# Sharing the rows of w_out over the DMA engines in another way, in a decode block of cached attention and gMLP

## The chip, the cores and the metric

One core of a Trainium2 chip runs the whole program. Its engines are TensorE (PE in the profile, with its weight loads as PEld), VectorE (DVE), ScalarE (ACT), GpSimd (POOL) and SyncE (SP, which here does nothing but issue transfers). Transfers between HBM and the core's SBUF run on 16 DMA engines. SP, ACT and GpSimd put transfers into queues; each transfer is cut into packets, and each DMA engine works off its own share of them in order. The metric is the time of one execution on the device in microseconds; lower is better.

## What is computed

```python
def _A_ref(x, k_cache, v_cache, wq, wo):
    q = (x @ wq).reshape(B, Sq, H, Dh).transpose(0, 2, 1, 3)
    scores = jnp.einsum('bhqd,bhkd->bhqk', q, k_cache) * Dh ** (-0.5)
    p = _softmax(scores, axis=-1)
    o = jnp.einsum('bhqk,bhkd->bhqd', p, v_cache)
    return o.transpose(0, 2, 1, 3).reshape(B, Sq, H * Dh) @ wo

def _B_ref(x, w_in, w_sp, b_sp, w_out):
    z = _gelu(jnp.einsum('bsd,df->bsf', x, w_in))
    z1 = z[..., :Fh]
    z2 = _layernorm(z[..., Fh:], axis=-1)
    g = jnp.einsum('ts,bsf->btf', w_sp, z2) + b_sp[None, :, None]
    return jnp.einsum('bsf,fd->bsd', z1 * g, w_out)

xn = _layernorm(x, axis=-1)
return x + _A_ref(xn, k_cache, v_cache, wq, wo) + _B_ref(xn, w_in, w_sp, b_sp, w_out)
```

Four sequences (B = 4) of one new token each (Sq = 1), D = 640, 32 heads of 128, 4096 cached positions; the gMLP has Fh = 864. All inputs and the output are bf16. The caches are 4 x 32 x 4096 x 128 elements each, 134 MB for K and as much for V; wq and wo are 5.2 MB each, w_in 2.2 MB, w_out (864 rows of 640 elements, 1280 B a row) 1.1 MB.

## The kernel before

The heads are taken in four groups of eight, and a unit is one group of one sequence: 16 units of K and 16 of V, each 128 partitions of 65,536 B (8.4 MB). A big SBUF tile `kv` has five slots of half a unit. The units follow one another in the order of `seq`: four K units first, then V and K in turn, and each load (`load_unit`, L174 to L181) is issued by SP as soon as what lay in its slots has been read. SP works through its list in order, so a load that waits holds back all loads behind it.

A K unit goes through eight steps of `emit_K`: VectorE transposes an eighth of it into one half of `w_words` (L425), TensorE multiplies it with the queries in `QZ` (L436). After four K units comes a softmax (L481 to L501), and then the V units (`emit_V`, L503 to L526): 64 matmuls each (L509), a masking and a sum on VectorE. Each group's result goes through a selection matmul (L531) and is multiplied with its quarter of wo (`o_mul`, L548 to L553). The sum over groups, the residual and the gMLP's result gather in one PSUM tile, `proj`; the last quarter's later part goes into `last`, and both are added for the output (L617).

At the start, SP issues wq (L119), w_in (L122) and w_out; then the first K unit. w_out does not come in one piece. `FA` = 3 rows lie on each of the 128 partitions (`w_out`, L126 and L127: two rows and one row, 8 partitions a DMA engine, so 24 rows an engine). The other 480 rows lie in `w_rest`, which is a view of `w_words` that VectorE first clears (L128), as up to `FR` = 17 rows on a few partitions. The table `PC` (L61) lists these pieces: first and last partition, rows a partition, and `k`, the number of groups into which the source's outermost axis is put. A transfer is spread over as many DMA engines as its groups allow, and `load_piece` (L131) uses that: piece 0 is 200 rows in five groups, piece 1 is 144 rows in three, both issued by SP; piece 2 is 136 rows in two groups and is issued by GpSimd. Just before piece 2, GpSimd issues a transfer of 14 short runs in seven groups into a tile `walk` that nobody reads (L141); `tc.issue_after` keeps the two in that order. [...] What the engines carry of w_out is therefore uneven: three have 112 rows, two 64, two 92, nine 24.

The gMLP runs while the first K unit is on its way. Its 864 columns are laid out in `FC` = `FA` + `FR` = 20 chunks of up to 128, in the same order as the rows of w_out: `z_ps` takes the first three chunks (L338, L339), `zr_ps` the pieces (L343), both for all five parts `c` of D. ScalarE applies gelu (L349 for the chunks, L357 and L360 for the pieces), VectorE and GpSimd normalise (L371 to L389), VectorE transposes (L390), and TensorE adds 2 x 20 products to `proj` (L403). `w_words` then becomes the place of the K transposes.

At the end SP issues the remaining quarters of wo (L570 to L572): the second and the third in one transfer each, the last in five.

```python
load_wo(NG - 3)
load_wo(NG - 2)
load_wo(NG - 1, (0, 2, 4, 6, 7, 8))
```

After them, `emit_proj` multiplies the second and third quarter (L591 to L595; the third in two halves, L593 and L595), and L599 to L614 the last.

The loads of SP and ACT share eight completion semaphores in turn. A load waits until the load that had its semaphore before it has landed.

Of the kernel before, what the change touches and what calls it, by code (L numbers as in the profile page):

```python
# [8 lines left out]
ACT = mybir.ActivationFunctionType  # L9
ALU = mybir.AluOpType  # L10
AX = mybir.AxisListType
F32 = mybir.dt.float32
BF16 = mybir.dt.bfloat16
# [3 lines left out]
def kernel(  # L17
# [19 lines left out]
    nc = tc.nc  # L37
    P = 128
    B, Sq, D = A_x.shape
    _, H, Sk, Dh = A_k_cache.shape  # L40
    assert Sq == 1 and B == 4 and Dh == P and D % P == 0
    DC = D // P
# [9 lines left out]
    NG = H // HG  # L52
# [1 line left out]
    G = HG * B  # L54
    F2 = B_w_in.shape[1]
    Fh = F2 // 2
    FA = 3
    FR = 17
    nf = FA * P

    PC = ((0, 20, 10, 5), (32, 44, 12, 3), (60, 68, 17, 2))  # L61
    f_at = [nf]
    for p0, p1, n, _ in PC:
        f_at.append(f_at[-1] + (p1 - p0) * n)
    assert Fh == f_at[-1]
    FC = FA + FR
    NOUT = A_wo.shape[1]
# [5 lines left out]
    const = ctx.enter_context(tc.tile_pool(name="const", bufs=1))  # L73
# [12 lines left out]
    def misc_ps(shape, dtype):  # L86
        misc_ctr[0] += 1
        return ps_m.tile(shape, dtype, tag="misc", name=f"misc{misc_ctr[0]}")
# [5 lines left out]
    n_p = (2 * TC + 1) * 16  # L94
    w_words = const.tile([P, max(2 * NKT + n_p, FR * NOUT // 2)], F32, name="w_words")
    kT_t = w_words[:, 0:2 * NKT].rearrange("p (i n) -> p i n", i=2)
    pT_t = w_words[:, 2 * NKT:2 * NKT + n_p].bitcast(BF16).rearrange("p (j r) -> p j r", r=32)

    def at_slot(i, n, off=0):
        return kv[:, i * SL + off:i * SL + off + n]  # L100
# [22 lines left out]

    w_out = at_slot(2, FA * NOUT, n_in).rearrange("p (c n) -> p c n", c=FA)

    nc.sync.dma_start(out=w_out[:, 0:2], in_=B_w_out[0:2 * P, :].rearrange("(p c) n -> p c n", p=P))  # L126
    nc.sync.dma_start(out=w_out[:, 2:3], in_=B_w_out[2 * P:nf, :].rearrange("(p c) n -> p c n", p=P))  # L127
    nc.vector.memset(w_words[:, 0:FR * NOUT // 2], 0.0)  # L128
    w_rest = w_words[:, 0:FR * NOUT // 2].bitcast(BF16).rearrange("p (c n) -> p c n", c=FR)

    def load_piece(eng, t):  # L131
        p0, p1, n, k = PC[t]
        return eng.dma_start(out=w_rest[p0:p1, 0:n].rearrange("p c n -> p (c n)"),
                             in_=B_w_out[f_at[t]:f_at[t + 1], :].rearrange("(r i c) n -> i r (c n)", i=k, c=n))

    NST = 256
    walk = const.tile([14, NST], BF16)

    load_piece(nc.sync, 0)
    load_piece(nc.sync, 1)  # L140
    sw = nc.gpsimd.dma_start(out=walk, in_=B_w_out[0:14, 0:NST].rearrange("(r i) n -> i r n", i=7))  # L141
    with tc.issue_after(sw.ins):
        load_piece(nc.gpsimd, 2)

    NB = 32 * FC
    z_at = n_in + FA * NOUT

# [26 lines left out]
    def load_unit(item):  # L174
        key, u = item
        g, b = divmod(u, B)
        cache = A_k_cache if key == "k" else A_v_cache
        src = cache[b, g * HG:(g + 1) * HG].rearrange("e (m t) d -> (e m) (t d)", t=T)
        c = cuts.get(item, (0, T))
        for t0, t1 in zip(c[:-1], c[1:]):  # L180
            nc.sync.dma_start(out=unit(item, t0, t1), in_=src[:, t0 * Dh:t1 * Dh])  # L181
# [5 lines left out]
    def load_wo(g, c_cuts=(0, HG)):  # L187
        for c0, c1 in zip(c_cuts[:-1], c_cuts[1:]):
            nc.sync.dma_start(out=wo_t[g][:, c0:c1, :], in_=wo_q[g][:, c0:c1, :])  # L189
# [30 lines left out]
    xnT = const.tile([P, DC, 32], BF16)  # L220
# [43 lines left out]
    for q in range(4):  # L264
        nc.gpsimd.tensor_copy(out=SelE[32 * q:32 * q + 32, :, q % 2, :],
                              in_=b8[32 * q:32 * q + 32, 8:8 + HP, None].to_broadcast((32, HP, P // HG)))
# [10 lines left out]
                          in_=ident_f[:].rearrange("p (q x c) -> p q x c", q=2, c=C2))  # L277
# [12 lines left out]
    for hf in range(NH):  # L290
        nc.tensor.matmul(proj[0:32, 0:NO2], lhsT=ident_bf[:XR, 1 - hf:33 - hf],
                         rhs=x_bf[:, hf * NO2:(hf + 1) * NO2], start=(hf == 0), stop=False)
# [4 lines left out]
    for hf in range(2):  # L297
        for c in range(DC):
            for j in range(NG):
                n0 = j * HG * Dh + hf * 512  # L300
                nc.tensor.matmul(q4_ps[32 * j:32 * j + 32, hf * 512:hf * 512 + 512], lhsT=xnT[:, c, :],  # L301
                                 rhs=wq[:, c, n0:n0 + 512], start=(c == 0), stop=(c == DC - 1))
# [12 lines left out]


    w_z = w_in.rearrange("p c (a f) -> p c a f", a=2)
    z_ps = misc_ps([P, 2, FA, 32], F32)
    zr_ps = misc_ps([P, 2, 256], F32)


    z_in = [[], [], [], []]
    for t, (p0, p1, n, k) in enumerate(PC):
        src = w_z[:, :, :, f_at[t]:f_at[t + 1]]
        for q in range(p0 // 32, (p1 - 1) // 32 + 1):
            x0, x1 = max(p0, 32 * q), min(p1, 32 * q + 32)
# [3 lines left out]
            else:  # L330
                src_q = src
            z_in[q].append((t, x0 - 32 * q, x1 - 32 * q, src_q))
    z_of = [[sum((x1 - x0) * PC[t][2] for t, x0, x1, _ in z[:m]) for m in range(len(z) + 1)] for z in z_in]
    w_z2 = w_z[:, :, :, 0:2 * P].rearrange("p c a (q j i) -> p c q a i j", q=4, j=32)
    w_z1 = w_z[:, :, :, 2 * P:nf].rearrange("p c a (q j) -> p c q a j", q=4)
    for c in range(DC):
        for q in range(4):
            nc.tensor.matmul(z_ps[32 * q:32 * q + 32, :, 0:2], lhsT=xnT[:, c, :], rhs=w_z2[:, c, q], start=(c == 0), stop=False)  # L338
            nc.tensor.matmul(z_ps[32 * q:32 * q + 32, :, 2], lhsT=xnT[:, c, :], rhs=w_z1[:, c, q], start=False,  # L339
                             stop=(c == DC - 1))  # L340
        for q in range(4):
            for m, (_, _, _, src) in enumerate(z_in[q]):
                nc.tensor.matmul(zr_ps[32 * q:32 * q + 32, :, z_of[q][m]:z_of[q][m + 1]], lhsT=xnT[:, c, :], rhs=src[:, c],  # L343
                                 start=(c == 0 and m == 0), stop=(c == DC - 1 and m == len(z_in[q]) - 1))
    z_f = at_slot(2, 2 * 3 * NB, z_at).bitcast(F32).rearrange("p (a n) -> p a n", a=3)
    z_b = at_slot(2, 2 * NB, z_at + 6 * NB).rearrange("p (a n) -> p a n", a=2)
    zT = z_f[:, 0:2, :].rearrange("p a (i j) -> p a i j", j=32)
    nc.gpsimd.memset(z_f[:, 0:2, :], 0.0)
    nc.scalar.activation(out=zT[:, :, 0:FA, :], in_=z_ps[:], func=ACT.Gelu_apprx_tanh)  # L349
    for q in range(4):  # L350
        rows = slice(32 * q, 32 * q + 32)
        for m, (t, x0, x1, _) in enumerate(z_in[q]):
            p0, p1, n, k = PC[t]
            z = zr_ps[rows, :, z_of[q][m]:z_of[q][m + 1]]
            dst = zT[rows, :, FA:FA + n, x0:x1]
            if x1 - x0 < p1 - p0:
                nc.scalar.activation(out=dst, in_=z.rearrange("p a (x c) -> p a c x", c=n), func=ACT.Gelu_apprx_tanh)  # L357
            else:
                for a in range(2):
                    nc.scalar.activation(out=dst[:, a].rearrange("p c (i r) -> p c i r", i=k),  # L360
                                         in_=z[:, a].rearrange("p (r i c) -> p c i r", i=k, c=n), func=ACT.Gelu_apprx_tanh)
# [36 lines left out]
    for f0 in range(0, FC, 4):  # L398
        for hf in range(NH):
            for fc in range(f0, min(f0 + 4, FC)):  # L400
# [3 lines left out]
                                 rhs=(w_out[:, fc] if fc < FA else w_rest[:, fc - FA])[:, hf * NO2:(hf + 1) * NO2],  # L404
                                 start=(fc == 1 and hf == 0), stop=False)
# [122 lines left out]
    def emit_sel(g):  # L528

        ox = misc_ps([P, B, P // HG, HG], F32)  # L530
        nc.tensor.matmul(ox[:].rearrange("p b q c -> p (b q c)"), lhsT=SelX[:].rearrange("p h q -> p (h q)"),  # L531
                         rhs=state["R"][:].rearrange("p b d -> p (b d)"), start=True, stop=True)
        om = ppool.tile([P, B, P // HG, HG], F32, tag="p", name="om")
        nc.vector.tensor_tensor(out=om[:], in0=ox[:], in1=MkQ[:, None, :, None].to_broadcast((P, B, P // HG, HG)), op=ALU.mult)
        state[("om", g)] = om
# [19 lines left out]
    def emit_proj(g, h2=range(2), close=False):  # L555
        for h in h2:
            for hf in range(NH):
                for c in range(4 * h, 4 * h + 4):
                    o_mul(proj[32 * (c % 2):32 * (c % 2) + 32], g, c, hf, hf * NO2, (hf + 1) * NO2, False,
                          close and c == HG - 1 and hf == NH - 1)  # L560

    fill_qz(0)
    for i, item in enumerate(seq):
        if i + 1 < len(seq):
            key, u = seq[i + 1]
            load_unit(seq[i + 1])
            if key == "k" and u == 2 * B - 1:
                load_wo(u // B - 1)
        else:
            load_wo(NG - 3)  # L570
            load_wo(NG - 2)
            load_wo(NG - 1, (0, 2, 4, 6, 7, 8))  # L572
        key, u = item
        g, b = divmod(u, B)
        if key == "k":
            done = b == B - 1 and g > 0
            for k in range(8):
                emit_K(u, k)
                if done and k == 1:
                    emit_sel(g - 1)  # L580
                if done and k == 2:
                    emit_oT(g - 1)
                if done and k == 5 and g == 1:
                    emit_proj(g - 1)
            if b == B - 1:
                if g < NG - 1:
                    fill_qz(g + 1)
                softmax(g)
        else:
            emit_V(u)  # L590
# [58 lines left out]
```

## Time and profile before

| | |
|---|---|
| median of 3 runs | 663.54 us (663.45 to 664.74) |
| the profiled execution | 663.36 us, of which the span on the engines is 661.6 us |
| busy in the span | VectorE 377.3 us (57%), TensorE 281.7 (43%), ScalarE 73.9 (11%), GpSimd 70.3 (11%) |
| first K load (L181) issued, landed | 17.95 us, 45.52 us |
| gMLP's products (L403) | 38.68 to 43.87 us |
| first K transpose (L425) | 45.74 us |
| K and V loads, issue to landing | 27.6 / 30.5 / 44.2 us (least, median, most) |
| TensorE clock granted, mean | 0.755 |

A page of the profile has six parts: busy times, the span in 40 slices, the DMA queues, the chain of work that ended last, the costliest groups of instructions, and the transfers. In the first part the shares are of the span. In the DMA part, q1 is SP's queue, q10 ScalarE's and q0 GpSimd's; q8 and q14 bring instructions to the engines. The chain of waits starts at the last instruction and goes back, at each step to what released it; in order of time its lines give start, duration and what it was. A row of the window table gives start and end, length, the busy time of each engine with its number of instructions, and at its end the granted clock, the busy share of the 16 DMA engines and GB/s.

### The profile page before, as it was taken

What the parts mean: (1) busy time and instruction counts of PE and PEld (TensorE: products, weight loads), DVE (VectorE), ACT (ScalarE), POOL (GpSimd) and SP (SyncE); (2) the same over time, 40 slices, a digit from 0 to 9 for tenths busy, and PEclk for the clock granted to TensorE, in tenths of its full rate; (3) what the DMA queues carried; (4) which work ended last, traced back from release to release, by engine and by line L of the source; (5) the groups of instructions that cost most, each with busy time, mean ns of one, the idle gap of its engine ahead of it and who ended that gap; (6) DMA issues with size and microseconds to landing.
All of it is one profiled execution on the core that took longest, in us unless ns stands there. A gap on an engine that the chain in (4) does not pass through costs nothing.

```text
span 661.6 us, 5513 instructions
## 1 busy us (share of the span) xinstructions
PE 281.7 (43%) x2293; PEld 106.9 (16%) x2293; DVE 377.3 (57%) x307; ACT 73.9 (11%) x143; POOL 70.3 (11%) x138
## 2 busy tenths in 40 slices
PE   0445555437052455334435075532606245652236
PEld 0221111112011121111112021110202112120012
DVE  4329989766191758718346196864629175971112
ACT  0300000330100000340200000070110000043200
POOL 3620000030200000130300000030020000003300
PEclk9868879778687697677759677875867778666779
DMA  8999999999999999999999999999999999999997
GB/s 367 458 421 440 425 436 445 436 421 440 421 436 437 444 405 436 441 441 436 433 420 428 437 422 445 442 425 432 432 433 432 433 440 411 446 432 429 423 423 286
DMA packets 7276, 282.60 MB, mean 427 GB/s; under 512 B 929, under 2 KB 1324, under 8 KB 1836
## 3 DMA queue, kind: packets, MB, share of 16 engines
q1 hardware_dynamic: 7112, 282.07, 98.9%
q8 instruction: 18, 0.29, 0.2%
q0 software_dynamic: 112, 0.18, 0.1%
q14 instruction: 6, 0.05, 0.0%
q10 hardware_dynamic: 28, 0.01, 0.0%
HBM read 282.25 MB, written 0.01 MB: 427 GB/s over the span
## 4 chain that ended last, share of the span: by engine, by line
DMA 74%; DVE 12%; issue 11%; PE 2%; ACT 0%; SPq 0%; DVEq 0%; ACTq 0%
DMA kv<-in_A_k_cache_dram 63%; DVE w_words L425 11%; DMA kv<-in_A_v_cache_dram 5%; DMA kv<-in_A_wo_dram 3%; DMA kv<-in_A_wq_dram 3%; PE O L509 1%; DVE w_words L491 0%; PE S L436 0%; DVE Zb L469 0%; DVE m L443 0%; PE last L552 0%; ACT p_bf L485 0%; SPq L189 0%; PE proj L552 0%; PE misc L447 0%
## 5 line engine op out<-in xcount | busy, mean ns | idle before, releaser
L425 DVE STREAM_TRANSPOSE w_words<-kv 128x2048 f32<-128x2048 f32 x128 | 282.8, 2275 | 127.2 <-DMA kv<-in_A_k_cache_dram 127.2
L436 PE MATMUL S<-w_words,QZ 128*32 128x512 bf16 x1024 | 183.3, 490 | 262.5 <-DVE w_words L425 262.5
L436 PEld LDWEIGHTS <-QZ 128*32 128x32 bf16 x1024 | 59.2, 110 | 384.3 <-issue 318.1
L509 PE MATMUL O<-kv,Zb 128*32 128x512 bf16 x1024 | 72.0, 443 | 57.6 <-DMA kv<-in_A_v_cache_dram 51.1
L473 ACT ACTIVATE Zb<-w_words,MkE 32x128 bf16<-32x128 bf16 x120 | 60.9, 508 | 117.2 <-PE O L509 103.3
L518 DVE TENSOR_TENSOR om<-O,Mk 128x512 f32<-128x512 f32 x15 | 10.4, 692 | 92.1 <-PE O L509 92.1
L471 POOL TENSOR_SCALAR Zb<-w_words,MkE 32x128 bf16<-32x128 bf16 x60 | 43.3, 722 | 138.6 <-PE O L509 118.0
L485 ACT ACTIVATE p_bf<-S,negmax 128x1024 bf16<-128x1024 f32 x4 | 4.5, 1114 | 401.5 <-DVE negmax L453 401.5
L509 PEld LDWEIGHTS <-Zb 128*32 128x32 bf16 x1024 | 33.3, 110 | 96.1 <-issue 66.5
L469 DVE TENSOR_SCALAR Zb<-w_words,MkE 32x128 bf16<-32x128 bf16 x76 | 24.9, 327 | 2.3
L411 POOL COPY QZ<-qT 32x32 bf16<-32x32 bf16 x16 | 5.0, 315 | 184.9 <-PE S L436 184.3
L519 DVE TENSOR_REDUCE R<-om 128x128 f32<-128x512 f32 x15 | 15.3, 1020 | 0.5
L496 POOL TENSOR_SCALAR rs<-MkB,rowsum 128x4 f32<-128x4 f32 x4 | 1.2, 296 | 112.2 <-ACT p_bf L485 112.2
L491 DVE STREAM_TRANSPOSE w_words<-p_bf 128x1024 bf16<-128x1024 bf16 (+1 forms) x8 | 9.6, 1240 | 5.9 <-ACT p_bf L485 4.1
L542 POOL MEMSET oT<- 128x66 bf16 x4 | 0.5, 146 | 98.0 <-PE proj L552 98.0
L443 DVE TENSOR_REDUCE m<-S 128x1 f32<-128x1024 f32 x4 | 4.9, 1224 | 6.1 <-PE S L436 6.1
L521 DVE TENSOR_SCALAR R<-O,Mk 128x128 f32<-128x128 f32 x1 | 0.4, 351 | 13.0 <-PE O L509 13.0
L531 PE MATMUL misc<-R,SelX 128*128 128x512 f32 x8 | 4.5, 644 | 7.2 <-DVE R L519 5.5
L301 PE MATMUL q<-kv,xnT 128*32 128x512 bf16 x40 | 4.5, 631 | 6.4 <-DVE xnT L222 6.4
L498 PE MATMUL misc<-rs,SelE 128*128 128x4 f32 x8 | 2.3, 364 | 10.4 <-POOL rs L496 10.4
L552 PE MATMUL proj<-kv,oT 128*8 128x320 bf16 x52 | 5.6, 352 | 1.2 <-DMA kv<-in_A_wo_dram 1.2
L128 DVE MEMSET w_words<- 128x5440 f32 x1 | 4.6, 4592 | 1.9 <-issue 1.9
(107 smaller groups left out, 87.9 us busy)
## 6 DMA issues: line engine op xcount, KB each, us to landing
kv<-in_A_k_cache_dram SPq DMA_DIRECT2D x8, 4096.0 KB, 30.2
kv<-in_A_v_cache_dram SPq DMA_DIRECT2D x1, 6144.0 KB, 28.6
kv<-in_A_wq_dram SPq DMA_DIRECT2D x1, 5120.0 KB, 17.2
kv<-in_A_wo_dram SPq DMA_DIRECT2D x3, 1280.0 KB
kv<-in_B_w_in_dram SPq DMA_DIRECT2D x1, 2160.0 KB, 22.7
kv<-in_A_v_cache_dram SPq DMA_DIRECT2D x1, 2048.0 KB
kv<-in_A_wo_dram SPq DMA_DIRECT2D x3, 320.0 KB, 22.7
kv<-in_B_w_out_dram SPq DMA_DIRECT2D x1, 320.0 KB, 23.0
```

Of the source, the lines that this page charges most:

```text
L411: nc.gpsimd.tensor_copy(out=QZ[r0:r0 + 32, :, :, :, 8 + 8 * hp], in_=qT[32 * g:32 * g + 32, NE * hp:NE * hp + NE].rearrange("p e a b -> p ...
L425: nc.vector.transpose(kT.rearrange("p (t r) -> p t r", r=32), kw)
L436: nc.tensor.matmul(S_ps[32 * q:32 * q + 32, i], lhsT=QZ[:, b, 2 * kh + w, e, w0:w0 + 32], rhs=kb[:, i, :, e, :, w], start=(b == 0 and k < ...
L443: nc.vector.tensor_reduce(out=m1[:], in_=S_ps[:].rearrange("p i t m -> p (i t m)"), axis=AX.X, op=ALU.max)
L469: nc.vector.tensor_scalar(out=dst, in0=src, scalar1=mk, scalar2=None, op0=ALU.mult)
L471: nc.gpsimd.tensor_scalar(out=dst, in0=src, scalar1=mk, scalar2=None, op0=ALU.mult)
L473: nc.scalar.activation(out=dst, in_=src, func=ACT.Copy, scale=mk)
L491: nc.vector.transpose(pT_t[:, j0:j1, :], blocks)
L509: nc.tensor.matmul(O_ps[32 * q:32 * q + 32, :, :], lhsT=Zb[b % 2][:, w].rearrange("p h c -> p (h c)"), rhs=vv[:, w * 4 * Dh:(w + 1) * 4 * ...
L518: nc.vector.tensor_tensor(out=om4[:], in0=O_ps[:], in1=Mk4[:, :, None].to_broadcast((P, 4, Dh)), op=ALU.mult)
L519: nc.vector.tensor_reduce(out=R, in_=om4[:].rearrange("p c d -> p d c"), axis=AX.X, op=ALU.add)
L552: nc.tensor.matmul(dst[0:nb, 0:n1 - n0], lhsT=state[("oT", g)][:, c0:c0 + nb], rhs=wo_t[g][:, c, n0:n1], start=start, stop=stop)
```

## The change

Two rows of w_out instead of three lie on each partition, in one load instead of two: 16 rows an engine. The other 608 rows are cut in another way. Pieces 0 and 1 are both 220 rows in five groups, on SP's queue; piece 2 is 120 rows in two groups on GpSimd's. A fourth piece of 48 rows on three partitions follows on GpSimd's queue, after a second walk of 12 short runs in six groups. Its source is written as two halves. The gMLP then has 18 chunks instead of 20, and the tiles that depend on it become narrower. The pieces' columns of `z` are put into `zr_ps` for pieces 0 and 1 and behind the first chunks in `z_ps` for the others. The third quarter of wo is loaded in two halves.

```diff
-    FA = 3
-    FR = 17
+    FA = 2
+    FR = 16
...
-    PC = ((0, 20, 10, 5), (32, 44, 12, 3), (60, 68, 17, 2))
+    PC = ((0, 20, 11, 5), (32, 52, 11, 5), (60, 68, 15, 2), (124, 127, 16, 1))
...
-    nc.sync.dma_start(out=w_out[:, 0:2], in_=B_w_out[0:2 * P, :].rearrange("(p c) n -> p c n", p=P))
-    nc.sync.dma_start(out=w_out[:, 2:3], in_=B_w_out[2 * P:nf, :].rearrange("(p c) n -> p c n", p=P))
+    nc.sync.dma_start(out=w_out, in_=B_w_out[0:nf, :].rearrange("(p c) n -> p c n", p=P))
...
-        return eng.dma_start(out=w_rest[p0:p1, 0:n].rearrange("p c n -> p (c n)"),
-                             in_=B_w_out[f_at[t]:f_at[t + 1], :].rearrange("(r i c) n -> i r (c n)", i=k, c=n))
+        src = B_w_out[f_at[t]:f_at[t + 1], :]
+        src = src.rearrange("(r i c) n -> i r (c n)", i=k, c=n) if k > 1 else src.rearrange("(h c) n -> h (c n)", h=2)
+        return eng.dma_start(out=w_rest[p0:p1, 0:n].rearrange("p c n -> p (c n)"), in_=src)
...
+    walk2 = const.tile([12, NST], BF16)
...
-        load_piece(nc.gpsimd, 2)
+        p78 = load_piece(nc.gpsimd, 2)
+    with tc.issue_after(p78.ins):
+        sw2 = nc.gpsimd.dma_start(out=walk2, in_=B_w_out[0:12, 0:NST].rearrange("(r i) n -> i r n", i=6))
+    with tc.issue_after(sw2.ins):
+        load_piece(nc.gpsimd, 3)
...
-    z_ps = misc_ps([P, 2, FA, 32], F32)
+    z_ps = misc_ps([P, 2, 256], F32)
     zr_ps = misc_ps([P, 2, 256], F32)
...
+    def z_at_ps(q, m):
+        t, x0, x1, _ = z_in[q][m]
+        o = 32 * FA if t > 1 else 0
+        return (z_ps if t > 1 else zr_ps)[32 * q:32 * q + 32, :, o:o + (x1 - x0) * PC[t][2]]
...
-            load_wo(NG - 2)
+            load_wo(NG - 2, (0, 4, 8))
             load_wo(NG - 1, (0, 2, 4, 6, 7, 8))
```

More of the change, by code (lines that the diff above doesn't have):

```diff
@@ L332 @@
             z_in[q].append((t, x0 - 32 * q, x1 - 32 * q, src_q))
-    z_of = [[sum((x1 - x0) * PC[t][2] for t, x0, x1, _ in z[:m]) for m in range(len(z) + 1)] for z in z_in]
-    w_z2 = w_z[:, :, :, 0:2 * P].rearrange("p c a (q j i) -> p c q a i j", q=4, j=32)
-    w_z1 = w_z[:, :, :, 2 * P:nf].rearrange("p c a (q j) -> p c q a j", q=4)
+    def z_at_ps(q, m):
+        t, x0, x1, _ = z_in[q][m]
+        o = 32 * FA if t > 1 else 0
+        return (z_ps if t > 1 else zr_ps)[32 * q:32 * q + 32, :, o:o + (x1 - x0) * PC[t][2]]
+    w_za = w_z[:, :, :, 0:nf].rearrange("p c a (q j i) -> p c q a i j", q=4, j=32)
     for c in range(DC):
         for q in range(4):
-            nc.tensor.matmul(z_ps[32 * q:32 * q + 32, :, 0:2], lhsT=xnT[:, c, :], rhs=w_z2[:, c, q], start=(c == 0), stop=False)
-            nc.tensor.matmul(z_ps[32 * q:32 * q + 32, :, 2], lhsT=xnT[:, c, :], rhs=w_z1[:, c, q], start=False,
-                             stop=(c == DC - 1))
+            nc.tensor.matmul(z_ps[32 * q:32 * q + 32, :, 0:32 * FA], lhsT=xnT[:, c, :], rhs=w_za[:, c, q], start=(c == 0),
+                             stop=(c == DC - 1 and all(z[0] < 2 for z in z_in[q])))
         for q in range(4):
-            for m, (_, _, _, src) in enumerate(z_in[q]):
-                nc.tensor.matmul(zr_ps[32 * q:32 * q + 32, :, z_of[q][m]:z_of[q][m + 1]], lhsT=xnT[:, c, :], rhs=src[:, c],
-                                 start=(c == 0 and m == 0), stop=(c == DC - 1 and m == len(z_in[q]) - 1))
+            for m, (t, _, _, src) in enumerate(z_in[q]):
+                nc.tensor.matmul(z_at_ps(q, m), lhsT=xnT[:, c, :], rhs=src[:, c], start=(c == 0 and t < 2), stop=(c == DC - 1))
     z_f = at_slot(2, 2 * 3 * NB, z_at).bitcast(F32).rearrange("p (a n) -> p a n", a=3)
@@ L348 @@
     nc.gpsimd.memset(z_f[:, 0:2, :], 0.0)
-    nc.scalar.activation(out=zT[:, :, 0:FA, :], in_=z_ps[:], func=ACT.Gelu_apprx_tanh)
+    nc.scalar.activation(out=zT[:, :, 0:FA, :], in_=z_ps[:, :, 0:32 * FA].rearrange("p a (i j) -> p a i j", j=32),
+                         func=ACT.Gelu_apprx_tanh)
     for q in range(4):
@@ L353 @@
             p0, p1, n, k = PC[t]
-            z = zr_ps[rows, :, z_of[q][m]:z_of[q][m + 1]]
+            z = z_at_ps(q, m)
             dst = zT[rows, :, FA:FA + n, x0:x1]
```

## The prediction

> **What bounds the kernel now.** I first read the page's DMA parts, then two stretches of the window table, then the end of the chain of waits.
>
> ```profile
> DMA  8999999999999999999999999999999999999997
> DMA packets 7276, 282.60 MB, mean 427 GB/s; under 512 B 929, under 2 KB 1324, under 8 KB 1836
> ## 3 DMA queue, kind: packets, MB, share of 16 engines
> q1 hardware_dynamic: 7112, 282.07, 98.9%
> q8 instruction: 18, 0.29, 0.2%
> q0 software_dynamic: 112, 0.18, 0.1%
> q14 instruction: 6, 0.05, 0.0%
> ```
> ```profile
> 40.00:300.00 260.00, 117.46 (x890) 44.02 (x886) 173.30 (x130) 28.79 (x56) 19.72 (x34) 0.78 1.00 434
> 300.00:630.00 330.00, 139.23 (x1104) 51.02 (x1108) 182.75 (x143) 36.95 (x72) 28.70 (x43) 0.72 1.00 432
> ```
> The last two figures of a window row are DMA share and GB/s. From 40 to 630 us all 16 DMA engines are busy, while TensorE and VectorE have slack: 117 and 173 us of work in 260 (the first and third figures). The kernel is the transfers, and it ends when the slowest DMA engine ends:
> ```profile
> 633.82 23.04 DMA kv<-in_A_wo_dram
> 656.86 0.04 issue
> 656.91 0.23 PE last L552
> 657.14 0.64 PE proj L552 x4
> 657.78 0.68 PE last L552 x15
> 658.46 0.04 issue
> 658.50 0.32 PE last L552 x4
> 658.82 0.02 issue
> 658.85 0.32 DVE o_bf L617
> ```
> The last piece of wo lands at 658.46; four matmuls, one VectorE addition and the store follow, and the span ends 3.1 us later. So the question is only which engine is last, and how much work it has.
>
> The views do not print this, but the trace holds every packet (start, duration, bytes) and the 16 arrivals of each load, one an engine. Packets follow each other on an engine without a gap, so an engine can be followed from its w_out packets onwards. Rows of w_out per engine before: 24 each from the first two loads; 40 more on five engines (four packets of 12800 B each), 48 more on three of those five (15360 B), 68 more on two others (21760 B). I call them A1 to A3 (112 rows), B1 and B2 (64), C1 and C2 (92), and nine others (24). At the first K load the arrivals show it, in us after the earliest, 40.60: seven others 0 to 0.36, two others 1.47 and 1.65 (one began 1.2 late, one had an instruction fetch), B 2.23 and 2.28, C 3.62 and 3.77, A 4.50, 4.81 and 4.92.
>
> Later the order changes, because of the instruction packets. Each of the 18 on q8 (16384 B, one about every 38 us) takes 0.98 to 1.10 us and the packet behind it 0.4 to 0.5 more: about 1.5 us on one engine. In turn they hit eight of the nine others, twice each by the end. The six on q14 (8192 B) cost 0.6 to 1.0. The one at 88.3 follows a packet of one of the two B engines, and with the next load that engine is at 3.21 instead of 2.28; the one at 278.8 hits the same engine (3.20 to 4.16), the one at 468.5 again (2.73 to 3.69; the earliest engine had in between moved 1.43). I call it B2. Even spacing of 190 us makes it the instruction stream of one engine, VectorE's by its number of instructions.
>
> At the first piece of wo's last quarter (earliest 652.37) the offsets are: one of the others, never hit, 0; B1 1.49; seven others 1.66 to 2.00; C 2.15 and 2.28; one other (third fetch) 3.26; A 3.31, 3.46 and 3.71; B2 3.67 to 3.71. Five engines end together, and B2 is one of the last, though it had 48 rows fewer than A.
>
> **The change, part by part.**
>
> *Rows moved.* A row costs 47.9 ns (12800 B, ten rows, in 479 ns). A: four packets of 10 and four of 12 rows (4 x 479 + 4 x 573 = 4.21 us) become eight of 11 rows (8 x 0.526 = 4.21): nothing. All engines lose a third row on each of eight partitions, 8 packets of 1280 B at 55 ns: -0.44. So A -0.44. B: four of 479 (1.92) become eight of 526 (4.21): +2.29 - 0.44 = +1.85. C: four of 808 (17 rows) become four of about 712 (15 rows): -0.38 - 0.44 = -0.82. Six others get a packet of the second walk (46 ns by the first walk's): -0.39. The last gets 48 rows, +2.29 - 0.44 = +1.85.
>
> *wo split (0, 4, 8).* Eight packets of 10240 B per engine become sixteen of 5120 B. At equal bytes that is between nothing and +0.2 us (10240 B take 388 ns, 2560 B take 102, so quartering costs 20 ns a packet, 0.16 for eight); halving is nearer the small end, +0.06 for every engine. TensorE can start eight of the sixteen L593/L595 matmuls earlier, but behind them the end waits for the last piece, as at 658.46 now: 0.
>
> *New ends.* B2 3.69 + 1.85 + 0.06 = 5.60. A at most 3.71 - 0.38 = 3.33; the thrice-fetched other 2.9; B1 3.4; the engine with 48 rows 1.9; C 1.5. The last engine is B2, 5.60 against 3.71 before: **+1.9 us**. No row is queued that this could hide behind: the engines have no idle time after it, and the tail hangs on the latest arrival.
>
> *gMLP, 18 chunks for 20.* Four L403 matmuls fewer (4.41 us for 33, so 0.5), and some 8.6 us of POOL and VectorE passes over 640 columns become 10% shorter (-0.8); two more gelu activations of 0.25 (+0.5). Hidden: L403 ends at 43.9, and what comes next on w_words is the K transposes, which start at 45.74 when K has landed (45.52; now about 45.1). 1.2 us of cover remain even with no saving; without it each us late would be a us late at VectorE, which has 87 us of slack in the 260 from 40 on.
>
> *Queues.* SP issues one load fewer at the start, and its first K load no longer waits for wq's completion semaphore (the eight are reused in turn, and the turn moves by one), so it is issued at about 9 instead of 17.95: nothing, since no engine is free before 20.8. In the tail, by the same turn, the last two pieces of wo wait for the two halves of the last V load (landing 644.18 and 649.06, +1.9) instead of being issued at 634.8 and 644.2. At 651.0 the last still has 4 us until the earliest engine needs it: 0; on B2 9 us. GpSimd issues two DMAs more after 6.82 (0.57 to 0.80 each); behind them stand ident_f and ones_f, then L211, which waits until 13.27 for VectorE: hidden.
>
> *Sum.* 663.36 (the profiled execution, span 661.6) + 1.9 = **665.2 us**; the median of the runs shown, 663.54, is 0.2 above this execution.
>
> [...]
>
> **Rivals.**
> 1. *B2 is relieved.* If in the new program the 190 us stream fetches through another engine, B2 ends at 2.7 and the A engines set the end at 3.33: -0.38, 663.0, not slower. It decides from two of the three fetches (0.95 each) being gone. For it: nothing in one trace tells what binds a stream to an engine, and q8's does change engines. Against: three of three hit B2, and VectorE's program has as many instructions as before.
> 2. *The last piece does not stay on one engine.* Three runs over three engines, two of them A: alone 665.2 as well; with rival 1 A ends at 3.71 + 0.38, 663.7. For it: three equal runs as built. Against: the two-fold piece did go to two.
> 3. *A fetch at the very end.* TensorE's last fetch starts at 655.92, with some 74 instructions left. The program is 36 shorter, so the same point comes amid the last pieces; a TensorE that waits for it loses up to 1.1: 666.3. Against: now it works on through the fetch.
> 4. *Better balance.* All 16 ends averaged are 2.3, so evening out perfectly gives -1.4, 661.9. Against: B and the 48-row engine both gain rows, only one of them had room.
>
> **How the numbers follow.** Forecast 0.66 (rival 2 is inside it where B2 is last), rival 1 with or without 2 0.24, rival 3 0.05, rival 4 0.05. The forecast's own range is 664.6 to 665.8 (split 0 to +0.2, the run's own spread). For 8 in 10 it reaches down to rival 1: 662.8 to 665.9. 0.2% is 1.3 us, about what measuring this kernel can tell from no change: slower 0.67, same 0.27, faster 0.06.
>
> **What would show it.** Right: the arrivals of the last wo pieces have one engine alone 1.5 to 2.3 us behind the next; the last arrival near 660.3; L403 still ends before the first K arrival; 24 instruction packets, three of the small ones on one of the five engines. Wrong: five or more engines arriving together at the end, or the five-fold pieces spread over other engines than the first five.

## The result: 666.67 us, and the profile after

The changed kernel takes 666.67 us (median of 6 runs, 666.09 to 667.28), the kernel before, run beside it on the same chip, 663.43. The ratio is 1.0047 with a 95% interval of 1.0037 to 1.0058: slower by 3.2 us, where 1.9 was forecast. The time lies above the range that was stated (662.8 to 665.9).

The page of the changed kernel looks like that of before. Its DMA parts (the second and third part of the page):

```profile
DMA  8999999999999999999999999999999999999995
DMA packets 7350, 282.61 MB, mean 425 GB/s; under 512 B 986, under 2 KB 1259, under 8 KB 2027
## 3 DMA queue, kind: packets, MB, share of 16 engines
q1 hardware_dynamic: 7122, 282.03, 98.6%
q8 instruction: 18, 0.29, 0.2%
q0 software_dynamic: 176, 0.23, 0.1%
q14 instruction: 6, 0.05, 0.0%
```

The same megabytes, and the same 18 and 6 instruction packets; GpSimd's queue (q0) carries 176 packets instead of 112. The last slice of the DMA row falls from 7 to 5: at the end more engines have run out of work. The end of the chain of waits (start, us, what), of the changed kernel:

```profile
652.90 9.37 DMA kv<-in_A_wo_dram
662.26 0.04 issue
662.31 0.32 PE last L560 x4
662.63 0.02 issue
662.65 0.32 DVE o_bf L625
```

The tail is the one of before, 3.8 us later: the last piece of wo lands at 662.26 instead of 658.46. (This profiled execution has a span of 665.4 us and took 667.28 us, at the upper end of its runs; by the medians the difference is 3.2.) Behind each large load the trace holds 16 arrivals, one an engine. Those of the last piece of wo, in us:

```
before  654.91 656.34 656.49 656.54 656.56 656.67 656.80 656.81 656.92 657.06 658.02 658.03 658.23 658.27 658.41 658.46
after   656.58 658.13 658.14 658.16 658.16 658.21 658.23 658.38 658.41 658.84 659.80 660.40 660.45 660.76 660.77 662.26
```

Two things are in these rows. One engine is now alone at the end, 1.49 behind the next: 5.68 behind the earliest, where the forecast had B2 at 5.60 behind the earliest engine of before. And the whole row has moved: the earliest engine, again one that no instruction fetch hits, ends 1.67 later, though it has eight rows fewer, which should have brought it forward by 0.4. Nothing in the forecast delays all engines at once.

The place of that second step is found from the start. The arrivals of w_in, all of whose packets are queued ahead of most of w_out, begin at 20.06 before and at 22.05 after; taken in order, each of the 16 is later, by 1.27 to 2.61. The window table there (start and end, length, PE, PEld, DVE, ACT and POOL busy with instructions, granted clock, DMA share, GB/s), first before, then after:

```profile
17.00:19.00 2.00, 0.86 (x12) 0.33 (x16) 1.05 (x4) 0.00 (x0) 1.64 (x8) 1.00 0.98 419
19.00:21.00 2.00, 2.00 (x24) 0.76 (x20) 0.00 (x0) 0.00 (x0) 2.00 (x9) 1.00 1.11 452
```
```profile
17.00:19.00 2.00, 0.00 (x0) 0.10 (x1) 1.03 (x3) 0.00 (x0) 1.63 (x8) 1.00 1.27 214
19.00:21.00 2.00, 1.22 (x12) 0.51 (x15) 0.00 (x0) 0.00 (x0) 2.00 (x9) 1.00 0.77 259
21.00:23.00 2.00, 2.00 (x24) 0.92 (x20) 0.00 (x0) 0.00 (x0) 1.79 (x6) 1.00 1.39 585
```

From 17 to 21 us the engines stay busy and deliver half: 214 and 259 GB/s instead of 419 and 452. (A packet's bytes are booked where it starts, so the row behind reads high.) The DMA view of that stretch, changed kernel, says what is under way:

```profile
DMA packets 50, 0.51 MB, mean 206 GB/s; under 512 B 21, under 2 KB 21, under 8 KB 21
## 3 DMA queue, kind: packets, MB, share of 16 engines
q1 hardware_dynamic: 26, 0.41, 101.0%
q0 software_dynamic: 24, 0.10, 17.5%
```

Only 26 packets of SP's queue start in 2.5 us on 16 engines. A packet of w_in (17280 B) takes 644 ns; here 27 of the 128 take over a tenth more, up to 2304 ns. Added up, the time above 644 is 1.65 us an engine on the mean of the 16; before it is 0.000. Of the 24 packets of GpSimd's queue that start in that stretch, three have 20480 B each, 16 rows: they start at 17.05 to 17.28 and go to partitions 124, 125 and 126. At w_in's rate one would take 0.76 us; they take 1.33, 1.80 and 1.81. They are the fourth piece of w_out.

So there are two suspects for 3.2 us: B2's 40 rows, which were forecast, and a stall of all engines around the fourth piece, which was not.

### The profile page after: what moved, and what is told of

It is laid out like the page before. It is cut to its first block, busy times and chain, and to the rows that moved or that the text cites. A ratio compares the mean times of both kernels' runs of the same rounds, so it can differ in the third digit from the quotient of the medians.

```text
span 665.4 us, 5483 instructions
## 1 busy us (share of the span) xinstructions
PE 289.2 (43%) x2274; PEld 108.9 (16%) x2274; DVE 377.0 (57%) x307; ACT 74.3 (11%) x145; POOL 70.5 (11%) x140
## 4 chain that ended last, share of the span: by engine, by line
DMA 76%; DVE 12%; issue 11%; PE 1%; SPq 0%; DVEq 0%
DMA kv<-in_A_k_cache_dram 65%; DVE w_words L433 11%; DMA kv<-in_A_v_cache_dram 9%; DMA kv<-in_A_wo_dram 1%; PE O L517 1%; DVE w_words L127 1%; SPq L134 0%; DVEq L433 0%; SPq L186 0%; PE last L560 0%; DVE o_bf L625 0%
## 5 line engine op out<-in xcount | busy, mean ns | idle before, releaser
L444 PE MATMUL S<-w_words,QZ 128*32 128x512 bf16 x1024 | 186.0, 496 | 257.9 <-DVE w_words L433 257.9
L517 PE MATMUL O<-kv,Zb 128*32 128x512 bf16 x1024 | 75.4, 460 | 57.6 <-DMA kv<-in_A_v_cache_dram 50.5
L542 DVE TENSOR_TENSOR om<-misc,h 128x512 f32<-128x512 f32 x4 | 2.8, 691 | 4.9 <-PE misc L539 4.9
```

The source lines that it names most:

```text
L444: nc.tensor.matmul(S_ps[32 * q:32 * q + 32, i], lhsT=QZ[:, b, 2 * kh + w, e, w0:w0 + 32], rhs=kb[:, i, :, e, :, w], start=(b == 0 and k < ...
L517: nc.tensor.matmul(O_ps[32 * q:32 * q + 32, :, :], lhsT=Zb[b % 2][:, w].rearrange("p h c -> p (h c)"), rhs=vv[:, w * 4 * Dh:(w + 1) * 4 * ...
```

## The experiments

"Excess" below is that sum over the packets of w_in above 644 ns, divided by 16 engines; "B2" and "A" are the engines as the prediction names them. The time before, beside these runs, was 663.35 to 663.38 us.

**no_rows48: the changed kernel without the fourth piece.** The second walk stays; 48 rows of w_out are left out.

```diff
-    with tc.issue_after(sw2.ins):
-        load_piece(nc.gpsimd, 3)
```

> The changed kernel without the load of its last piece (48 rows of w_out are left out, their partitions stay zero); the second walk stays. Theory: the 3.2 us lost are two terms, 1.9 for the 40 rows more on B2 and 1.9 for a stall of all 16 DMA engines around 17 to 20 us, while three engines write the 48 rows into three neighbouring partitions. Then this is 664.8, and the rate from 17 to 19 us is back at 410 to 420 GB/s instead of 214. Rival 1, all of it is B2 being later than reckoned: 666.7. Rival 2, the stall comes from the second walk: 666.7 and the rate stays low.

Measured: 665.18 us (665.10 to 665.30), ratio 1.0027 [1.0017, 1.0036]. The stall is gone (excess 0.001, and the window row reads as before):

```profile
17.00:19.00 2.00, 0.77 (x8) 0.42 (x12) 0.66 (x2) 0.00 (x0) 1.68 (x8) 1.00 0.97 417
```

B2 stays alone at the end: 660.30, the next 658.25. What is left, 1.8 us above before, is close to the forecast's whole sum; the fourth piece is worth 1.49 by the medians. That is less than the 1.9 that was expected of it, so the time came out 0.4 above the expected 664.8. Between the profiled executions, B2's last arrival differs by 1.96 (662.26 and 660.30).

**b_back: the changed kernel with B as before.** Piece 1 goes to three engines of four partitions instead of five; 88 rows are left out, 44 on each B.

```diff
-    load_piece(nc.sync, 1)
+    nc.sync.dma_start(out=w_rest[32:44, 0:11].rearrange("p c n -> p (c n)"),
+                      in_=B_w_out[f_at[1]:f_at[1] + 132, :].rearrange("(r i c) n -> i r (c n)", i=3, c=11))
```

> The changed kernel with piece 1 loaded in three groups of 44 rows, so that B1 and B2 have 60 rows of w_out instead of 104 (88 rows are left out). The last piece of 48 rows stays. Theory of two terms: B2 ends 2.1 earlier and is no longer last; the end is set by the next engines, 1.5 before it in the changed kernel's last arrivals (660.77 against 662.26): 665.2. Rival 1, all of it is B2: 663.4. Rival 3, all of it is the stall: 666.7.

Measured: 665.87 us (665.57 to 666.02), 1.0035 [1.0022, 1.0047], 0.7 above the expected 665.2. (The expectation took its 1.5 from the changed kernel's profiled execution, which is 0.6 above the median; and the engines next in line end at 661.03 here, not at 660.77.) The stall is there:

```profile
17.00:19.00 2.00, 0.16 (x4) 0.23 (x8) 1.18 (x4) 0.00 (x0) 1.64 (x8) 1.00 1.19 275
19.00:21.00 2.00, 2.00 (x24) 0.79 (x20) 0.00 (x0) 0.00 (x0) 2.00 (x9) 1.00 0.76 260
```

Excess 1.21. And the three engines with the 48 rows can now be told: the last three arrivals of the first K load are 47.40, 47.42 and 47.97, 5.8 to 6.3 behind the earliest (41.63), and the next before them is 44.94. A, which the change's other rows leave where it was, had 4.5 to 4.9 there; all three A engines are 0.9 to 1.8 later, none is left at its old place, and 16 rows are 0.77. So the fourth piece went to A1, A2 and A3.

**both_out: both edits above.** 136 rows are left out.

> Both edits: the last piece is not loaded and B1 and B2 have 60 rows (136 rows left out). Theory of two terms: back to before, less the 0.4 that the A engines save with 8 rows fewer: 663.0 to 663.2. If something else in the change costs time (18 chunks, the split of wo, the order of the completion semaphores): above 663.6.

Measured: 663.15 us (663.03 to 663.38), 0.9994 [0.9985, 1.0003], as expected. The four cases together, in us:

| | B with 104 rows | B with 60 rows |
|---|---|---|
| with the fourth piece | 666.67 | 665.87 |
| without it | 665.18 | 663.15 |

B's 44 rows cost 2.03 without the piece (44 rows at 47.9 ns are 2.1) and 0.80 with it; the piece costs 1.49 with B2 last and 2.72 without. The terms don't add because the end is the latest of 16 engines: in the left column B2 is last and pays the stall but no rows, in the lower right A is last (by the forecast's sum), and in the upper right A pays the stall, its own stretched packets and 16 rows (by b_back's packets, 1.21 on the mean of the engines, 0.25 to 1.35 above 0.76, and 0.77).

**What makes the stall.** It could be the rows' number, GpSimd's queue, or where the rows are written. Four kernels vary these. *half_shared* puts 8 rows instead of 16 on each of the three partitions (24 rows left out). *own_groups* writes three times 16 rows without the second walk and to partitions 68, 72 and 76, four apart; it was meant for three engines other than A, which the author took to write these partitions in the large loads (no run shows that), but in the trace each of the three packets is followed on its engine by eight packets of pieces 0 and 1, as on A and B alone, and the last arrivals point to A again (these 48 rows are left out of the product). *sp_issue* issues the whole piece from SP instead, behind piece 1, with no second walk. *half_own* puts the 8 rows on partitions 0, 4 and 8, in a free part of `kv` (all 48 rows left out of the product); the same assumption gives these partitions to the A engines.

```diff
  half_shared
...
-        load_piece(nc.gpsimd, 3)
+        nc.gpsimd.dma_start(out=w_rest[124:127, 0:8].rearrange("p c n -> p (c n)"),
+                            in_=B_w_out[f_at[3]:f_at[3] + 24, :].rearrange("(p c) n -> p (c n)", p=3))
...
  own_groups
...
+        nc.gpsimd.dma_start(out=w_rest[68:77:4, 0:16].rearrange("p c n -> p (c n)"),
+                            in_=B_w_out[f_at[3]:f_at[3] + 48, :].rearrange("(p c) n -> p (c n)", p=3))
...
  sp_issue
...
+    nc.sync.dma_start(out=w_rest[124:127, 0:16].rearrange("p c n -> p (c n)"),
+                      in_=B_w_out[f_at[3]:f_at[3] + 48, :].rearrange("(p c) n -> p (c n)", p=3))
...
  half_own
...
+        nc.gpsimd.dma_start(out=at_slot(1, 8 * NOUT, 11264)[0:9:4],
+                            in_=B_w_out[f_at[3]:f_at[3] + 24, :].rearrange("(p c) n -> p (c n)", p=3))
```

> The changed kernel with the last piece half as long: 8 rows on each of partitions 124 to 126 (24 rows are left out). Theory, the stall lasts as long as three engines write into the one group of partitions 124 to 127: about half of what the 48 rows cost (1.5 in time against the kernel without them, 1.65 us of excess on the w_in packets per engine), so 665.9 to 666.1 and 0.8 us of excess. Rival, the stall is a fixed cost of this transfer: 666.7 and 1.65.

> The changed kernel without the second walk, its last piece in the same three runs of 16 rows, now on partitions 68, 72 and 76 (rows of w_out that no column of z meets, so they count as left out). [...] Theory that the stall is three engines writing into partitions that one engine's share has: no stall, 17 to 19 us near 415 GB/s, B2 last: 664.8 to 665.1. Rival, a transfer of 20480-byte packets on three engines stalls wherever it goes: 666.7.

> The changed kernel without the second walk and with the last piece (48 rows into partitions 124 to 126, all rows loaded) issued by SP behind pieces 0 and 1 instead of by GpSimd. Theory that the destination makes the stall: the same stall, but when the A engines get there, around 27 to 30 us, and 666.5 to 666.8. Rival, it is GpSimd's queue that stalls the engines: 665.2.

> [...] The three engines are the A engines: in the run without the B rows all three A engines were 0.8 later than 104 rows explain, none of the others. Theory that a stall needs an engine that writes outside its own group of four partitions: no stall, 665.2 as without the rows, 17 to 19 us at 417 GB/s. Rival, any such three-row transfer of GpSimd's stalls all engines: as the half piece, 665.9 or more.

| run | the three packets | they took, ns | excess, us an engine | earliest arrival of w_in | median, us |
|---|---|---|---|---|---|
| before | none | | 0.000 | 20.06 | 663.4 |
| after | 20480 B, partitions 124 to 126 | 1325, 1801, 1806 | 1.65 | 22.05 | 666.67 |
| half_shared | 10240 B, the same partitions | 385, 385, 460 | 0.59 | 20.75 | 665.71 |
| own_groups | 20480 B, partitions 68, 72, 76 | 901, 1027, 1068 | 0.51 | 20.78 | 665.96 |
| sp_issue | 20480 B, partitions 124 to 126 | 1371, 1381, 1926 | 0.000; on the first K load's packets 1.70 | 20.04 | 667.05 |
| half_own | 10240 B, partitions 0, 4, 8 | 385, 385, 385 | 0.001; on the first K load's 0.001 | 20.18 | 676.15 |

half_shared (1.0035 [1.0022, 1.0048]) and own_groups (1.0037 [1.0024, 1.0050]) come out between no_rows48 and after. half_shared lies 0.2 below its expected time and at 0.59 of excess for 0.8, far from the rival's 666.7 and 1.65. own_groups, expected without a stall on the assumption above, missed by 0.9. Its window:

```profile
17.00:19.00 2.00, 0.00 (x0) 0.10 (x1) 0.69 (x2) 0.00 (x0) 1.65 (x8) 1.00 0.82 330
```

The stall grows with the bytes (0.59 with 10240 B a packet, 1.65 with 20480), and at 20480 B it is smaller with three partitions four apart (0.51) than with three neighbouring ones (1.65). In half_shared packets that themselves take little over the 385 ns of half_own's hold up all the others: the earliest arrival of w_in is 0.7 late. The windows of half_shared:

```profile
17.00:19.00 2.00, 0.46 (x8) 0.31 (x12) 0.68 (x2) 0.00 (x0) 1.64 (x8) 1.00 0.94 275
19.00:21.00 2.00, 2.00 (x24) 0.82 (x20) 0.00 (x0) 0.00 (x0) 2.00 (x9) 1.00 0.94 395
```

sp_issue (1.0056 [1.0043, 1.0070]; 0.25 above its expected range) acquits GpSimd's queue and the second walk. w_in passes untouched, the three packets run at 24.7 to 24.9 us, and the stall moves there with them:

```profile
17.00:19.00 2.00, 0.97 (x12) 0.58 (x16) 0.73 (x3) 0.00 (x0) 1.64 (x9) 1.00 0.97 416
...
25.00:27.00 2.00, 0.13 (x2) 0.09 (x1) 0.00 (x0) 1.84 (x4) 1.31 (x5) 1.00 0.86 262
27.00:29.00 2.00, 0.16 (x1) 0.00 (x0) 0.55 (x2) 1.95 (x8) 0.34 (x1) 0.83 0.54 229
```

half_own missed its expected time by 11 us (1.0192 [1.0178, 1.0206]), for a reason of its own making: its transfer into `kv` waits on GpSimd for w_in,

```profile
23.68 0.62 POOL L148 DMA_DIRECT2D kv<-in_B_w_out_dram  x1 [6.82 <-DMA kv<-in_B_w_in_dram]
```

and the first step on x, which needs `kv`, waits for that transfer in turn: on VectorE it starts at 33.19, where before it starts at 11.11.

```profile
33.19 1.59 DVE L211 CAST kv<-kv 8x640 f32<-8x640 bf16 x1 [27.00 <-DMA kv<-in_B_w_out_dram]
```

The second K load is then issued at 48.31 instead of 25.62, and the DMA engines run dry between 40 and 80 us (269 and 332 GB/s).

```profile
40.00:60.00 20.00, 6.39 (x88) 3.29 (x88) 5.78 (x13) 6.97 (x15) 7.40 (x10) 0.79 0.66 269
60.00:80.00 20.00, 12.86 (x92) 5.55 (x93) 17.34 (x9) 0.00 (x0) 0.00 (x0) 0.87 0.80 332
```

Its time says nothing on the question, but its packets do: at 29.6 us, amid the first K load as in sp_issue, with half_shared's bytes, all three take 385 ns and nothing around them is stretched. The destination is what neither of those two has in common with it. The length of the packets is not enough for a stall either: the kernel before has eight of 21760 B in GpSimd's queue, on partitions 60 to 67, each 808 ns, with an excess of 0.000.

**one_row: the rows where they cost least, all of them, four partitions a group.** One row instead of two lies on each partition (FA = 1, FR = 17), and GpSimd's queue carries 17 rows a partition in two groups and then 9 rows a partition in seven groups, on partitions 68 to 95; no second walk, wo as before.

```diff
...
-    PC = ((0, 20, 11, 5), (32, 52, 11, 5), (60, 68, 15, 2), (124, 127, 16, 1))
+    PC = ((0, 20, 9, 5), (32, 44, 14, 3), (60, 68, 17, 2), (68, 96, 9, 7))
...
```

> A kernel with all rows, made from what the runs show: one row on each partition instead of two (8 rows an engine), pieces 0 and 1 of 9 and 14 rows a partition in five and three groups, 17 rows in two groups, and in place of the second walk and the 48 rows a piece of 9 rows on partitions 68 to 95 in seven groups, each engine into its own four partitions; wo as before. Rows per engine: A 100, B 44, C 76, five to seven others 8 + 36. From the ends before (A 3.71, B2 3.69, thrice-fetched other 3.26, others up to 2.0, C 2.28): A 3.08, B2 2.7, others up to 2.9. Theory: the end moves by -0.6 from before, 662.7 to 662.8. Rival, a seven-group transfer of GpSimd's stalls the engines as well: 663.4 or more.

Measured: 664.24 us (663.99 to 664.32), 1.0012 [1.0003, 1.0020]: a miss by 1.5. By its time alone the rival (663.4 or more) would hold; the packets rule it out, for there is no stall: 28 packets of 11520 B, each 432 ns, excess 0.0000. The miss is balance. One engine is alone at the end, 659.37 against 657.84 for the next. The instruction fetch at 634 us lifts it from 2.7 to 4.25 behind the earliest. The account that fits is that it is the engine with the third fetch and one of the seven that got 36 rows: 3.26 before, less 0.82 for the rows taken away, plus 1.72 for 36 rows, gives 4.16 on the scale of before, 0.45 above the 3.71 that ended there. The last arrival moved by 0.91 (658.46 to 659.37), so half of it stays without an account. The expectation had not put the third fetch on one of the seven.

**four_own: the same with room left for that engine.** FA = 2, FR = 17, and the fourth piece is 8 rows a partition on four engines.

```diff
...
-    PC = ((0, 20, 11, 5), (32, 52, 11, 5), (60, 68, 15, 2), (124, 127, 16, 1))
+    PC = ((0, 20, 10, 5), (32, 44, 12, 3), (60, 68, 17, 2), (68, 84, 8, 4))
...
```

> All rows of w_out are loaded and used. Two rows lie on each partition (16 an engine), pieces 0 and 1 are 200 and 144 rows on SP's queue as before, GpSimd's queue carries 136 rows in two groups and then 128 rows in four groups on partitions 68 to 83 (32 rows each on four engines that have only 16 otherwise); no second walk, wo's quarters as before. Each engine then has its rows of before less 8, four of them plus 24. Theory (rows plus instruction fetches, and no stall as long as an engine writes its own partitions): packets of the fourth load (10240 B) at their nominal 385 ns, w_in's packets with no excess; ends of A at 3.33, B2 at 3.31, the engine with the third fetch at 2.9 unless it is one of the four, then 4.0; so 663.0 (663.38 - 0.38), or 663.7 if the thrice-fetched engine is one of the four. Rival (a fourth load on GpSimd's queue costs a stall whatever partitions it writes): above 664.3, with w_in's packets delayed.

Measured: 663.16 us (663.05 to 663.26), 0.9997 [0.9988, 1.0006], 0.2 above the expected 663.0. 16 packets of 10240 B, each 385 ns; excess 0.000; the window is the one of before:

```profile
17.00:19.00 2.00, 0.88 (x12) 0.48 (x16) 0.48 (x2) 0.00 (x0) 1.64 (x9) 1.00 1.00 426
```

At the end seven engines arrive between 657.64 and 658.14, none alone. This fourth load on GpSimd's queue, to partitions 68 to 83, makes no stall. The version is better than the changed kernel by 3.5 us, and not distinguishable from the kernel before.

## Where the prediction was right and which step failed, point by point

*The bound and the way to the end: right.* The transfers bound the kernel after as before, and the tail behind the last arrival is 3.1 us again (662.26 to 665.4).

*B2: right, with its size.* The forecast had B2 last and alone, at 5.60 on a scale that starts at the earliest engine of before, read at the first piece of wo's last quarter. That engine was itself to come 0.38 earlier, which makes 5.98 behind the new earliest; at the same piece it is 5.84 (654.03 and 659.87). Its extra rows alone are worth 2.03 for 44 (no_rows48 against both_out), and no_rows48, which has B2's rows and no stall, is 1.8 above before where 1.9 was the sum. Rival 1 is out: B2 was not relieved. Of the signs named, the lone engine came true (1.49 behind the next, just under the 1.5 to 2.3; 2.05 in no_rows48) and so did the 24 instruction packets; the last arrival was to be near 660.3 and is 662.26, while no_rows48 ends at 660.30.

*The gMLP, the queues, the tail: right at nothing.* The first K load is issued at 7.97 instead of 17.95, with no gain; the last two pieces of wo are issued at 648.01 and 652.90 and nothing waits for that. The gMLP's products (L411 now) end at 46.34 and the K transposes begin at 48.31, when K has landed (48.02). The sign "before the first K arrival" was put badly: the earliest engine arrives at 42.20, but what counts is that all have landed. The cover is there: here K is late too, and in both_out, without the stall, the products end at 42.73 and K has landed at 45.08. both_out, which has all these parts, is 0.23 faster than before (0.38 was the sum for its A engines), inside what can be told.

*The fourth piece: the step that failed.* The sum had "The last gets 48 rows, +2.29 - 0.44 = +1.85", and rival 2 put the piece on three engines at "alone 665.2 as well". No run shows that a walk decides which engines the next transfer gets, on which the +1.85 for one engine rested; the runs put the piece on three engines, as rival 2 said, and they were not two but all three A engines (0.9 to 1.8 later in b_back), among the four engines that stand 3.97 to 4.39 behind the earliest at the first piece of wo's last quarter, where rival 2's 3.71 + 0.38 = 4.09 is 4.47 on this scale. Nor did the number of groups tell the engines: before, the pieces in five and three groups arrive five and three times (23.23 to 23.78, 25.50 to 26.07), while the fourth, with its source in two halves, came as three packets of 20480 B. All the forecast priced was rows on an engine, and the sum put what the piece does to the other engines at nothing, without a reason. The missing term was of that kind: while the three packets were written, the packets of w_in took 1.65 us more on the mean of the 16 engines, and B2, which has none of the piece's rows, ended later with the others. By the medians the piece costs 1.49 in the changed kernel, which is the gap between no_rows48 and after, and just what the forecast lacked (666.67 - 665.2 = 1.5). It alone puts the time outside the range.

*What the stall is, and what stays open.* Shown: it follows the piece and not the walk (excess 0.001 in no_rows48), and not GpSimd's queue (1.70 in sp_issue); it grows with the bytes on the same partitions (0.59 in half_shared, 1.65 after); it differs with the partitions written (with 10240 B a packet 0.59 in half_shared, 0.001 in half_own and 0.000 in four_own; with 20480 B 1.65 after, 0.51 in own_groups). That each engine has partitions of its own in the large loads, and that writing another's makes the stall, was the author's assumption: no view prints which engine writes which partitions, and no run shows it. The runs do not speak against it. Packets to partitions 68 to 95 in seven groups (one_row) and to 68 to 83 in four (four_own) cost 0.000, three to 68, 72 and 76 from the A engines (own_groups) cost 0.51, so the partitions alone do not decide; but the first two also have shorter packets (11520 and 10240 B against 20480). If three neighbouring partitions together take no more than one engine delivers (17280 B in 644 ns), three packets of 20480 B are 2.29 us of writing to them, an estimate. They took 2.04 from the first start to the last end (2.16 in sp_issue), but half_shared's three took 0.74 where this gives 1.15, so a shared limit is argued here and not shown. Why the thirteen engines without a packet of the piece wait as well is not shown by any run. Three partitions four apart (own_groups, 0.51) gave a third of the stall of three neighbouring ones (after, 1.65); what lies between, or whether one such packet alone costs anything, was not tried. The time with the stall also varies: the six executions of the changed kernel spread over 1.19 us, the nine of no_rows48 over 0.20.

## What to carry to other kernels

When a DMA-bound kernel's small loads are shared out by hand, add up each engine's rows and instruction fetches, and give the next row to the engine that ends earliest: one_row ended 0.9 us later than before, alone on one engine that an instruction fetch hit late. Price a load's destination beside its bytes: three packets of 20480 B to partitions 124 to 126 held up the loads in flight on all 16 engines (1.65 us an engine), and 28 of 11520 B to partitions 68 to 95 did not (0.0000). And ask the arrivals which engines a moved piece really uses; its place in the queue did not tell.

## What the hardware showed that was not expected

Three packets of 20480 B, 0.02% of the bytes, cut the load rate of the 16 engines together from 419 and 452 to 214 and 259 GB/s in two stretches of 2 us when they went to three neighbouring partitions (excess 1.65 us an engine); half the bytes cost 0.59, the same bytes to partitions 68, 72 and 76 0.51, half the bytes to partitions 0, 4 and 8 0.001. Nothing makes the time up afterwards: the earliest arrival of w_in is 1.99 us late at 22 us, and the earliest of the last piece of wo 1.67 late at the end, with eight rows fewer in between.

The second is where the small three-row transfer fell. The sum had put it on one engine with no walk's packet and no other piece. By the arrivals it fell on the A engines with the second walk (after), without it (own_groups) and from SP's queue (sp_issue). In the kernel before, the first walk's seven packets of 1024 B lie on seven engines and the eight of 21760 B of the two-group piece on two others, C1 and C2; no run leaves that walk out, so whether it decides this is not shown.
